# Batch sums of a feature-map attention with values as weights and Gram matrices for its key sums, and a re-searched hand order of the jobs

## The chip, the cores and the metric

The program runs on one core of a Trainium2 chip: TensorE (PE; its weight loads are listed apart, as PEld), VectorE (DVE), ScalarE (ACT), GpSimd (POOL) and SyncE (SP, which issues DMAs). The metric is the device time of one execution in microseconds. Each kernel is executed several times and the median counts; on one core the slowest core is the only one.

## The reference

Two blocks run one behind the other, for 4 batches of 1088 rows. The first is an attention without softmax over features phi, the outer product of two 8-wide sketches of a row; the second is a causal attention with 4 experts, of which each row uses two.

```python
def phi(x):
    a = np.einsum('rd,bhsd->bhsr', S1, x)
    b = np.einsum('rd,bhsd->bhsr', S2, x)
    return np.einsum('bhsi,bhsj->bhsij', a, b).reshape(*x.shape[:-1], r * r)
q_p, k_p = (phi(q), phi(k))
kv = np.einsum('bhsf,bhsd->bhfd', k_p, v)          # 64 x 32 per head
z = np.sum(k_p, axis=2)                            # 64 per head
num = np.einsum('bhsf,bhfd->bhsd', q_p, kv)
den = np.einsum('bhsf,bhf->bhs', q_p, z)[..., None] + 1e-06
x = num / den                                      # heads side by side: 1088 x 128
...
for e in range(E):                                 # 4 experts
    scores = scale * (x @ wq[e]) @ (x @ wk[e]).T   # causal
    a = softmax(scores)
    ye = a @ (x @ wv[e]) @ wo[e]
    out += (weight of e for the row, top 2 of x @ w_gate) * ye
```

All of it is float32. The sum z of a head's features is the 8x8 matrix of the sums over rows of a_i * b_j, and b is the row times S2, so z needs only sums over rows of products of two sketches.

## The kernel before

The kernel is a list of 1284 jobs (a `job(...)` call gives a name, the engines that may do it, what it reads, makes and holds). The order of the jobs is not worked out in the program: a table `ORDER` names them one after the other, with a letter for the engine where there is a choice, and `Plan.run` emits the instructions in that order. Each engine runs its own instructions in that order, so the table is the program's schedule; buffers go round in it too (`pools`: 4 pairs of PSUM banks called `pair`, 6 working tiles `w`, 3 feature tiles `fp`, 2 turned score tiles `AT` and so on).

The jobs of one batch, with the lines that the prediction speaks of:

- Loads of k, q and v, turned by DVE (`turn k`, `turn q`).
- `sketch k` (L523): 32x32 weights from the tables SK, 288 columns moving, 16 tiles of PE's array at a time. Where the weights hold both sketches of the split tables side by side, one pass over the data is enough and a job `join` adds the parts (batches 2 and 3); for batch 1 the tables are used one after the other and nothing is joined. `back` turns the sketches (DVE), `features` (L537, POOL or DVE) multiplies them out to 64 features per head.
- `sums` (L627): for each of 9 blocks of 128 rows and each of 4 heads one matmul with the 128x64 features as weights and 33 columns of v (the 33rd is 1.0 and gives z). `keep sums` copies kv and z to SBUF. `expand` (POOL) spreads z, `fifth` (L768) turns z into an 8-column table that makes the denominator a part of `sketch q`, and `repeat sums` (L762) puts kv into all four row groups of `kvr`. So `sketch q` of a batch stands behind the batch's whole sum. Constants for this (`pick8`, `rep4`, `rep16`, `repeat S2` on L362) are made at the start.
- `sketch q`, weights by the denominator on POOL and DVE, features, `turn f` (L805, DVE), then `numer` (L827), which gives x turned; `keep x`, `turn rows`, store and fetch of x through HBM.
- `logits` (L878, batch 0 L884) and the choice of experts on DVE; masks go through HBM (`store masks`, `fetch masks`) and land in `mb`.
- `query` (L1066), `base` and `pick` (L1079, DVE) give the chosen queries `qs` for three groups of tiles (6, 6 and 5 tiles of 64 rows); `score` (L1104) and `take` (L1116), `exp` (ACT), `guard`, `invert`, `weigh` (L1147, POOL), `turn A` (L1152, DVE) give a tile's weights; `sum V` (L1180) adds them up for a whole group with 32x128 weights, four row tiles of the array at a time; `keep V`, `patch V`, `spread V` choose the experts' parts and `out` (L1301, L1251, L1277) projects.

Batch 0 differs: its attention is done by rows (`project`, `sums 0`, L619, `turn qf`, L666, `numer 0`, L692), and it is the only work there is at the start. `spread v` copies its values into the layout of the sums (L193, ACT and POOL).

PE's matmuls use its array in different shapes: whole (128x128: queries, scores, outputs, transposes), 32x128 (sum V, repeat sums), 128x64 (sums, fifth), 128x32 (logits), 32x32 (sketches, numer). A float32 matmul of the program is two passes in the trace, so the counts of the trace are twice those of the code.

## Time and profile before

| what | value |
|---|---|
| median of 3 runs | 262.74 us (262.19 to 263.94) |
| the profiled execution's span | 261.8 us, 9228 instructions |
| PE busy | 254.9 us (97%), 3811 matmul passes |
| DVE busy | 208.4 us (80%), 529 instructions |
| POOL busy | 157.5 us (60%) |
| ACT busy | 105.6 us (40%) |
| granted clock of PE | 0.9 or more in all 40 slices of the span |

The profiled execution is one of its own; its span runs from the first to the last instruction, and the runs' times hold a little more around it (the median is 0.94 us above the span). A stretch of PE that is counted as busy may still hold short waits, since matmuls are pipelined.

### The profile page before, as it was taken

The page shows a single profiled execution, that of the slowest core. Times are in us where ns is not written, and L with a number is a line of the kernel's source. Part 1 is how long each engine was busy: PE and PEld are TensorE (multiplying, and loading weights), DVE is VectorE, ACT ScalarE, POOL GpSimd, SP SyncE. Part 2 cuts the span into 40 slices and gives each one's busy share as a digit, 9 for nine tenths or more (in the row PEclk, how much of TensorE's full clock was granted, in tenths as well). Part 3 has the DMA queues.
Part 4 walks back from the last instruction along what each step waited for, and adds up shares of the span by engine and source line. Part 5 has one row for each costly group of instructions (what it writes and reads, how often), then busy time and mean ns, then how long its engine had stood idle before and what let it go on. Part 6 is the DMA issues. An engine that isn't in the chain of part 4 may idle for free.

```text
span 261.8 us, 9228 instructions
## 1 busy us (share of the span) xinstructions
PE 254.9 (97%) x3811; PEld 192.2 (73%) x3811; DVE 208.4 (80%) x529; ACT 105.6 (40%) x279; POOL 157.5 (60%) x266
## 2 busy tenths in 40 slices
PE   7899999999999999999999999999999999999995
PEld 2787666646958887665897986666689875589994
DVE  5778999999998996998887497998994388893442
ACT  3453354757242225532814044635514215723120
POOL 5546776899578716597467682366273842542642
PEclk9999999999999999999999999999999999999999
DMA  7978689891467275906044685003370379240012
GB/s 149 212 122 186 112 207 168 158 146 20 73 135 166 67 184 114 148 4 183 3 84 83 143 167 120 4 3 90 93 120 4 96 141 238 47 96 3 5 30 59
DMA packets 87739, 27.35 MB, mean 104 GB/s; under 512 B 58576, under 2 KB 87056, under 8 KB 87696
## 3 DMA queue, kind: packets, MB, share of 16 engines
q1 hardware_dynamic: 85184, 26.15, 50.7%
q10 hardware_dynamic: 2512, 0.61, 1.0%
q8 instruction: 30, 0.49, 0.8%
q14 instruction: 13, 0.11, 0.2%
HBM read 22.22 MB, written 4.52 MB: 102 GB/s over the span
## 4 chain that ended last, share of the span: by engine, by line
PE 84%; DMA 8%; DVE 5%; POOL 1%; issue 1%; SPq 0%; ACT 0%; DVEq 0%; POOLq 0%; ACTq 0%
PE pair L1180 28%; PE pair L1104 24%; PE pair L1066 9%; PE pair L1301 7%; DMA mb<-md 4%; PE pair L1251 3%; PE pair L523 2%; PE pair L827 2%; DMA in<-in_q_dram 2%; DMA w<-in_v_dram 2%; PE pair L627 2%; DVE w L1116 1%; PE pair L1277 1%; DVE fp L805 1%; PE pair L619 1%; PE pair L692 1%
## 5 line engine op out<-in xcount | busy, mean ns | idle before, releaser
L1147 POOL TENSOR_SCALAR w<-w,rs,sh 128x256 f32<-128x256 f32 (+14 forms) x68 | 56.8, 840 | 34.4 <-DVE rs L1143 32.8
L1104 PE MATMUL pair<-xT,qs 128*128 128x320 f32 (+9 forms) x216 | 74.0, 478 | 0.4 <-DVE qs L1079 0.4
L1132 ACT ACTIVATE w<-w,mx 128x64 f32<-128x64 f32 (+15 forms) x68 | 52.4, 772 | 45.8 <-DVE mx L1116 40.6
L1116 DVE CUSTOM_DVE_ANT_0 w<-pair,mask 128x64 f32<-128x64 f32 (+14 forms) x68 | 48.3, 723 | 15.4 <-PE pair L1104 13.0
L1104 PEld LDWEIGHTS pair<-xT,qs 128*128 128x128 f32 x216 | 38.8, 190 | 25.9 <-issue 11.1
L1152 DVE STREAM_TRANSPOSE AT<-w 128x320 f32<-128x320 f32 (+15 forms) x68 | 51.2, 762 | 3.4 <-POOL w L1147 3.0
L1180 PEld LDWEIGHTS pair<-AT,xra 32*128 32x128 f32 x1136 | 41.6, 185 | 4.6 <-issue 2.0
L1180 PE MATMUL pair<-AT,xra 32*128 32x160 f32 (+5 forms) x1136 | 44.9, 303 | 0.0
L1207 POOL TENSOR_TENSOR agg<-agg,mb 128x768 f32<-128x768 f32 (+1 forms) x22 | 34.0, 1559 | 3.4 <-DVE agg L1203 2.0
L1066 PE MATMUL pair<-xT,Mq 128*128 128x384 f32 (+1 forms) x96 | 34.0, 475 | 0.0
L193 ACT COPY agg<-pair 128x384 f32<-128x384 f32 (+1 forms) x31 | 13.2, 463 | 45.5 <-PE pair L1180 44.0
L1180 PEld LDWEIGHTS pair<-AT,xrb 32*128 32x128 f32 x752 | 26.4, 185 | 2.4 <-issue 2.2
L1180 PE MATMUL pair<-AT,xrb 32*128 32x160 f32 (+5 forms) x752 | 28.0, 289 | 0.0
L1140 POOL TENSOR_SCALAR rs<-zs 128x1 f32<-128x1 f32 x32 | 6.8, 214 | 34.0 <-ACT w L1132 23.5
L1066 PEld LDWEIGHTS pair<-xT,Mq 128*128 128x128 f32 x96 | 17.3, 190 | 10.3 <-issue 3.2
L1079 DVE COPY_PREDICATED qs<-mb,pair 128x768 f32<-128x768 uint16 (+1 forms) x24 | 23.1, 962 | 1.5 <-ACT qs L193 0.3
L537 POOL TENSOR_TENSOR fp<-w 128x576 f32<-128x576 f32 x19 | 22.6, 1209 | 1.6 <-DVE w L527 1.1
L1301 PEld LDWEIGHTS pair<-Mo,agg 128*128 128x128 f32 x168 | 20.6, 192 | 2.4 <-issue 0.5
L1301 PE MATMUL pair<-Mo,agg 128*128 128x128 f32 x168 | 21.4, 277 | 0.0
L193 ACT COPY qs<-pair 128x384 f32<-128x384 f32 (+1 forms) x21 | 9.2, 463 | 19.5 <-PE pair L1066 14.2
L1203 DVE COPY_PREDICATED agg<-mb,pair 128x384 f32<-128x384 uint16 (+1 forms) x24 | 12.7, 557 | 4.8 <-ACT agg L193 4.4
L1132 ACT ACTIVATION_READ_ACCUMULATOR w<-w,mx 128x1 f32 x68 | 12.8, 189 | 0.0
(179 smaller groups left out, 297.2 us busy)
## 6 DMA issues: line engine op xcount, KB each, us to landing
xra<-xd SPq DMA_DIRECT2D x16, 192.0 KB, 5.2
xrb<-xd SPq DMA_DIRECT2D x16, 192.0 KB, 5.4
xrc<-xd SPq DMA_DIRECT2D x16, 160.0 KB, 5.0
mb<-md SPq DMA_DIRECT2D x4, 576.0 KB, 7.4
mb<-md SPq DMA_DIRECT2D x4, 480.0 KB, 4.4
mb<-md SPq DMA_DIRECT2D x6, 288.0 KB, 4.3
in<-in_k_dram SPq DMA_DIRECT2D x12, 136.0 KB, 3.4
in<-in_q_dram SPq DMA_DIRECT2D x3, 544.0 KB, 5.6
```

The source lines that it names most:

```text
L193: (nc.scalar.copy if eng == "ACT" else VEC[eng].tensor_copy)(o, i)
L537: VEC[e].tensor_tensor(out=f, in0=a[:, :, None, R : 2 * R].to_broadcast([128, j1 - j0, R, R]), in1=a[:, :, 0:R, None].to_broadcast([128, j ...
L1066: nc.tensor.matmul(plan[ps[x]][:, y, 0:w], Mq[:, ((1, 2), (0, 3))[x][y]], plan[xT][:, 64 * t0 : 64 * t1], start=True, stop=True)
L1079: nc.vector.copy_predicated(chosen(), rows(c), rows(plan[ps[x]]))
L1104: nc.tensor.matmul(plan[p][:, y, 0 : c1 - c0], plan[qs][:, 128 * t : 128 * t + 128], plan[xT][:, c0:c1], start=True, stop=True)
L1116: nc.vector.tensor_tensor_reduce(out=o, in0=src, in1=msk, scale=-1.0, scalar=mx[:, b, i, x - 1 : x] if x else 3e38, op0=ALU.add, op1=ALU.m ...
L1132: nc.scalar.activation(out=a, in_=a, func=ACTF.Exp, bias=mx[:, b, i, last : last + 1], scale=-1.0, accum_out=zs[:, b, i : i + 1])
L1147: nc.gpsimd.tensor_scalar(out=a, in0=a, scalar1=rs[:, b, i : i + 1], scalar2=plan[("sh", b)][:, i : i + 1], op0=ALU.mult, op1=ALU.mult)
L1152: nc.vector.transpose(dst[:, 0 : keys // 32, t], plan[A][:, 0:keys].rearrange("p (j s) -> p j s", s=32))
L1180: nc.tensor.matmul(plan[Vk[g // 2]][:, g % 2, lo : 32 * nt], plan[(f"xr{j // 12}", b)][rows, j % 12], a[rows, j, lo:], start=(j == 0), sto ...
L1207: nc.gpsimd.tensor_tensor(out=a, in0=a, in1=plan[mb][:, 2 * x : 2 * x + 2, 0:w], op=ALU.mult)
L1301: nc.tensor.matmul(plan[p][0:m, 0, 128 * x : 128 * x + 128], plan[agg][:, e, 128 * x : 128 * x + m], Mo[:, e], start=(e == 0), stop=(e == ...
```

## The change

The sums of batches 1 to 3 are done the other way round. `kv` takes 32 columns of v as weights and 64 features as moving columns, four heads at a time in the four column groups of the array. z no longer comes from it: `gram` multiplies the sketches of k with themselves (weights 32 columns, 8 moving columns per head and row block), `tables` turns the result into the denominator's table with a constant SB, and `sketch q` waits for these two only, not for the sum. `repeat kv` takes kv in two halves per head. Batch 1's `sketch k` becomes the one-pass form with a `join`. The constants for the old way go; SB is made from SD on POOL and DVE.

```diff
-        def sums(m):
-            t = plan[kvb][:, :, 0 : D + 1]
+        def sums():
             kp = plan[fps["k"]].rearrange("p (j h f) -> p j h f", h=H, f=R * R)
             for j in range(NJ):
-                for x in range(2):
-                    h = 2 * m + x
-                    nc.tensor.matmul(t[64 * x : 64 * x + 64, m], kp[:, j, h], plan[vp][:, j, h, :],
+                for h in range(H):
+                    nc.tensor.matmul(plan[kvb][32 * h : 32 * h + 32, 0, 0 : R * R], plan[vp][:, j, h, 0:D], kp[:, j, h],
                                      start=(j == 0), stop=(j == NJ - 1))
+        def gram():
+            a = parts_ab("k")
+            for j in range(NJ):
+                for h in range(H):
+                    nc.tensor.matmul(plan[zb][32 * h : 32 * h + 32, 0, 0:R], a[:, h, j], a[:, h, j, 0:R], start=(j == 0), stop=(j == NJ - 1))
...
+            job(f"gram {b}", "PE", 0.58, lambda e: gram(), [("ab", "k", b, 0), ("ab", "k", b, 1)], ("gram", b), [ab["k"], zb], mode="L", rank=at - 0.1)
...
         def repeat_sums():
-            for r in range(4):
-                rows = slice(32 * r, 32 * r + 32)
-                nc.tensor.matmul(plan[rep[r // 2]][:, r % 2, 0 : 2 * D], rep4[rows].rearrange("p g f -> p (g f)"),
-                                 plan[kvs][rows, :, 0:D], start=True, stop=True)
+            for h in range(H):
+                rows = slice(32 * h, 32 * h + 32)
+                for i in range(2):
+                    nc.tensor.matmul(plan[rep[h // 2]][:, h % 2, 32 * i : 32 * i + 32],
+                                     plan[kvs][rows, i].rearrange("p g f -> p (g f)"), ident[rows, rows], start=True, stop=True)
         def fifth():
-            for m in range(2):
-                for s in range(2):
-                    nc.tensor.matmul(plan[rep[0]][64 * m : 64 * m + 64, 0, 128 : 128 + R], S2r[:, s].rearrange("p x d -> p (x d)"),
-                                     zx[:, m], start=(s == 0), stop=(s == 1))
+            for s in range(2):
+                for h in range(H):
+                    nc.tensor.matmul(plan[zb][32 * h : 32 * h + 32, 1, 0:R], SB[:, s, 32 * h : 32 * h + 32], plan[zt],
+                                     start=(s == 0), stop=(s == 1))
...
-        job(f"expand {b}", "POOL", 0.35, lambda e: expand(), [("kvs", b), "pick8"], ("zx", b), [kvs], rank=at)
...
-            sketches("k", at, lambda: SK[:, 0:32] if b == 1 else None, (), lead_fp)
+            sketches("k", at, lambda: None, (), lead_fp)
```

The table `ORDER` is new from the first line on; its first words before and after:

```diff
-0 1 2 3 4 78 79 83 15a 80 45 21a 48 46 10a 81 90 53b 52b 91 54b 50 25b 18a 49 55b 5b 12a 14a 51 82 84 87 85 86 94 64
+0 1 2 3 4 76 77 81 15a 78 45 21a 48 46 10a 79 88 53b 52b 89 54b 50 25b 18a 49 55b 5b 12a 14a 51 13b 9a 11b 65 80 27b
```

What the table does to PE's and ACT's order is shown at three places.

The first is PE's order at the sums of batch 2. Before, the logits of batch 1 (L878), the sums of batch 2 (L627) and the sum V of batch 0's middle group (L1180):

```order
L1104 MATMUL pair_63<-xT_84,qs_97 128x448 x2
L878 MATMUL pair_64<-xT_85,wg 32x288 x4
L627 MATMUL pair_65<-vp_70,fp_77 64x33 x36
L1180 MATMUL pair_66<-AT_98,xra_86 128x192 x2
L1180 MATMUL pair_63<-AT_98,xra_86 128x192 x2
```

After, gram (L610), two scores (L1088), tables (L753), logits (L862), kv (L601) and sketch q (L499):

```order
L610 MATMUL pair_64<-w_73 32x8 x36
L1088 MATMUL pair_63<-xT_85,qs_98 128x480 x2
L753 MATMUL pair_64<-zt_82,SB 32x8 x8
L862 MATMUL pair_65<-xT_86,wg 32x288 x4
L601 MATMUL pair_66<-fp_79,vp_70 32x64 x36
L499 MATMUL pair_64<-in_68,skx_84 32x288 x8
L499 MATMUL pair_63<-in_68,skx_84 32x288 x8
```

The sums' 36 matmuls of 64 weight columns have become 36 of gram and 36 of kv, both in 128x32 form, beside the logits that have this form too; the sketch of q follows at once, where before that whole sum V, L762 and L768 lay between.

The second is PE's order in the sum V of batch 0's last group. Before, a score of batch 1 (L1104) stands inside it:

```order
L1180 MATMUL pair_65<-AT_99,xrb_87 128x160 x2
L1180 MATMUL pair_64<-AT_99,xrb_87 128x160 x2
L1104 MATMUL pair_63<-xT_85,qs_95 128x384
L1180 MATMUL pair_65<-AT_99,xrb_87 128x160 x2
L1180 MATMUL pair_64<-AT_99,xrb_87 128x160 x2
```

After, the same score (128x384) and two queries (L1050) stand ahead of it and the sum (L1164) is in one piece:

```order
L1088 MATMUL pair_64<-xT_86,qs_96 128x64
L1088 MATMUL pair_63<-xT_86,qs_96 128x192
L1088 MATMUL pair_66<-xT_86,qs_96 128x384
L1050 MATMUL pair_65<-xT_86,Mq 128x384 x2
L1164 MATMUL pair_64<-AT_100,xra_87 128x160 x2
L1164 MATMUL pair_63<-AT_100,xra_87 128x160 x2
```

The two changes of the array's shape around the single score are gone. Along the whole of PE's order, neighbours of different shape are 80 before and 62 after; from `numer 1` (the first rows of L827, now L811) to the end they are 50 and 38.

The third is the start. PE before, from the first numerators (L692) to the last logits of batch 0 (L884), with sketch k of batch 1 (L523), the weight products (L401), transposes (L707) and a query (L1066):

```order
L692 MATMUL pair_65<-kvz_80,fp_79 64x66 x12
L523 MATMUL pair_64<-in_68,SK 32x288 x8
L523 MATMUL pair_66<-in_68,SK 32x288 x8
L523 MATMUL pair_64<-in_68,SK 32x288 x8
L523 MATMUL pair_66<-in_68,SK 32x288 x8
L707 MATMUL pair_65<-ident,w_75 128x128 x3
L692 MATMUL pair_63<-kvz_80,fp_79 64x66 x12
L692 MATMUL pair_64<-kvz_80,fp_79 64x66 x12
L884 MATMUL pair_66<-xT_84,wg 32x192 x4
L401 MATMUL pair_65<-AT_98 128x128 x4
L401 MATMUL pair_63<-AT_98 128x128 x4
L707 MATMUL pair_64<-ident,w_75 128x128 x3
```

After, from the middle of that place (sketch k is now two rows) to the last logits (L868), with gram of batch 1 (L610):

```order
L693 MATMUL pair_63<-ident,w_76 128x128 x3
L678 MATMUL pair_65<-kvz_80,fp_78 64x66 x12
L678 MATMUL pair_64<-kvz_80,fp_78 64x66 x12
L868 MATMUL pair_66<-xT_85,wg 32x192 x4
L377 MATMUL pair_63<-AT_99 128x128 x4
L693 MATMUL pair_65<-ident,w_76 128x128 x3
L693 MATMUL pair_64<-ident,w_76 128x128 x3
L610 MATMUL pair_66<-w_71 32x8 x36
L377 MATMUL pair_63<-AT_99 128x128 x4
L868 MATMUL pair_65<-xT_85,wg 32x192 x4
L868 MATMUL pair_64<-xT_85,wg 32x160 x4
```

Sketch k has lost its second half, while gram of batch 1 and one of the two products have moved in ahead of the last logits. ACT's order at the copies of batch 0's values (`vp`, which L619 waits for), before:

```order
L193 COPY w_73<-pair_63 128x320
L193 COPY S2r<-pair_64 64x2x32 x2
L193 COPY vp_70<-w_72 64x4x9x32
L193 COPY w_74<-pair_65 128x192
L193 COPY w_74<-pair_66 128x384
```

and after:

```order
L194 COPY w_73<-pair_63 128x320
L194 COPY w_74<-pair_64 128x192
L194 COPY vp_70<-w_72 64x4x8x32
L194 COPY vp_70<-w_72 64x4x9x32
L194 COPY w_74<-pair_65 128x384
```

The copy of rows 64 to 127 (8x32 per head), which POOL did, now stands on ACT ahead of the other.

Two more moves of the table matter. Between `numer 1` and `numer 2` PE no longer has the output projections of batch 0's middle group (3 jobs, L1301), two queries of batch 1 and the scores of its tiles 7 and 11; they stand behind `numer 2` now. And all eight `features` jobs of q in batches 2 and 3 are POOL's now; DVE did five of them. On SP, `fetch masks` of batch 0 stands behind one `fetch x` and one `store x` that it was ahead of or beside.

## Rows read from the trace of the kernel before

**Rows 1.** The page, busy time, share of the span and instructions of each engine.
```profile
PE 254.9 (97%) x3811; PEld 192.2 (73%) x3811; DVE 208.4 (80%) x529; ACT 105.6 (40%) x279; POOL 157.5 (60%) x266
```

**Rows 2.** Windows: busy time of each engine in four stretches, us from the span's start.
```profile
core 0: us, PE busy (x) PEld busy (x) DVE busy (x) ACT busy (x) POOL busy (x), PEclk, DMA share, GB/s
29.90:52.40 22.50, 21.79 (x324) 14.91 (x321) 21.46 (x61) 11.22 (x37) 16.82 (x43) 1.00 0.87 159
52.40:101.00 48.60, 48.60 (x803) 36.80 (x814) 44.90 (x109) 19.21 (x51) 35.29 (x53) 1.00 0.60 116
101.00:157.90 56.90, 56.90 (x948) 43.78 (x960) 46.01 (x112) 22.79 (x62) 39.42 (x57) 1.00 0.48 98
157.90:258.60 100.70, 100.66 (x1416) 77.62 (x1415) 72.41 (x176) 38.77 (x100) 48.75 (x71) 1.00 0.34 72
```

**Rows 3.** Waits of PE's matmuls behind the first 10 us: us in total, times, longest.
```profile
PE pair L619 <- POOL vp L193: 0.9, 1, 0.9
...
PE pair L1104 <- DVE qs L1079: 0.4, 1, 0.4
PE pair L827 <- DVE w L527: 0.3, 1, 0.3
```

**Rows 4.** Chain that ended last, batches 1 and 2: start us, us, what.
```profile
52.37 2.16 PE pair L827 x42
...
63.21 2.22 PE pair L627 x72
...
70.67 0.22 PE pair L762 x4
...
72.67 0.34 PE pair L768 x8
...
97.44 1.78 PE pair L1301 x16
...
100.08 0.89 PE pair L1301 x8
100.97 1.48 PE pair L827 x38
```

**Rows 5.** The same chain: sketches with two tables and one, numerators of batch 0.
```profile
19.16 1.53 PE pair L523 x63
...
21.16 1.56 PE pair L692 x48
...
105.47 0.70 PE pair L523 x32
```

**Rows 6.** The same chain: 384 columns in whole-array form, inside such work, and between sums.
```profile
84.40 0.65 PE pair L1066 x2
...
91.56 0.84 PE pair L1104 x2
```

**Rows 7.** First passes of sum V (L1180) behind a query, 85.8 to 86.1 us: ns min/median/max.
```profile
L1180 PE MATMUL pair<-AT,xra x7: 294/398/398, 85.8 to 86.1; 32*128 32x160 f32 x7
```

**Rows 8.** ACT's timeline at the copies of batch 0's values.
```profile
10.44 1.17 ACT L193 COPY vp<-w 64x1152 f32<-64x1152 f32 x1
```

**Rows 9.** POOL's timeline at the same place.
```profile
11.09 1.83 POOL L193 COPY vp<-w 64x1024 f32<-64x1024 f32 x1 [1.22 <-DMA w<-in_v_dram]
```

**Rows 10.** DVE's timeline from 32 to 53 us, four of its pieces.
```profile
32.12 0.69 DVE L494 STREAM_TRANSPOSE in<-in 128x512 f32<-128x512 f32 x1
...
42.67 0.88 DVE L1079 COPY_PREDICATED qs<-mb,pair 128x640 f32<-128x640 uint16 x1 [0.24 <-DMA mb<-md]
...
49.31 0.92 DVE L1116 CUSTOM_DVE_ANT_0 w<-pair,mask 128x768 f32<-128x768 f32 x1
...
51.58 1.41 DVE L527 STREAM_TRANSPOSE w<-pair 128x576 f32<-128x576 f32 x2
```

**Rows 11.** Lines: the features on POOL and on DVE, busy us, mean ns of one.
```profile
L537 POOL TENSOR_TENSOR fp<-w 128x576 f32<-128x576 f32 x19 | 22.6, 1209 | 1.6 <-DVE w L527 1.1
...
L537 DVE TENSOR_TENSOR fp<-w 128x576 f32<-128x576 f32 x5 | 3.9, 802 | 0.8 <-POOL w L801 0.8
```

More of the change, by code (lines that the diff above doesn't have):

```diff
@@ L70 @@
+1281 1127b 1128 1123a 1129 1280 1130 1131 1132a 1136b 1137a 1134b 1133b 1135b
 """.split()
@@ L374, with keep_tables, widen_tables @@
-    job("keep S2", ("ACT", "DVE"), (2 * a_us(64), 2 * d_us(64)), lambda e, t=("ps", "S2"): keep_s2(e, t), ["S2p", "pick8"], "S2r",
-        [("ps", "S2")], rank=-29)
+    def keep_tables():
+        nc.gpsimd.tensor_copy(plan[("skx", 1)], SK[:, 0:32])
+    wide = ("w", "tables")
+    def widen_tables():
+        a = plan[wide][:, 0:256].rearrange("p (x h y) -> p x h y", x=2, h=H)
+        nc.gpsimd.memset(a, 0.0)
+        nc.gpsimd.tensor_copy(a[:, :, :, R : 2 * R], SD[:, :, :, R : 2 * R])
+    job("skx", "POOL", 0.25, lambda e: keep_tables(), ["SKW"], "skx", [("skx", 1)], rank=-31)
@@ L377, in one_hot @@
+    job("widen S2", "POOL", 0.6, lambda e: widen_tables(), ["SD"], "S2w", [wide], rank=-30)
+    job("turn S2", "DVE", 0.18 + 0.265, lambda e: nc.vector.transpose(SB.rearrange("p x y -> p (x y)"), plan[wide][:, 0:256]), ["S2w"], "SB",
+        [wide], rank=-29)
     def one_hot():
@@ L640, in prepare @@
                 [("fp", "k" + "+" * y, b, 0), ("vp", b), "const"] + [("kv0", b)] * y, ("kv", b) if y else ("kv0", b), [fps["k"], vp, kvb], mode="M", rank=at + 0.01 * y)
-        for m in range(0 if early else 2):
-            job(f"sums {b}.{m}", "PE", 1.3, lambda e, m=m: sums(m), [("fp", "k", b, m), ("vp", b), "const"],
-                ("kv", b), [fps["k"], vp, kvb], mode="M", rank=at)
-        kvs = ("kvs", b)
+        kvs, zt = ("kvs", b), ("zt", b)
+        if not early:
+            job(f"gram {b}", "PE", 0.58, lambda e: gram(), [("ab", "k", b, 0), ("ab", "k", b, 1)], ("gram", b), [ab["k"], zb], mode="L", rank=at - 0.1)
+            job(f"keep gram {b}", ("ACT", "DVE"), (a_us(8), d_us(8)), lambda e: copy(e, plan[zt], plan[zb][:, 0, 0:R]), [("gram", b)],
+                ("zt", b), [zb, zt], rank=at - 0.1)
+            job(f"kv {b}", "PE", 1.06, lambda e: sums(), [("fp", "k", b, 0), ("fp", "k", b, 1), ("vp", b), "const"],
+                ("kv", b), [fps["k"], vp, kvb], mode="L", rank=at)
         if early:
@@ L779, in attend_turned @@
-        job(f"repeat sums {b}", "PE", 0.25, lambda e: repeat_sums(), [("kvs", b), "rep4"], ("rep", b), [kvs, *rep], mode="V", rank=at)
-        job(f"fifth {b}", "PE", 0.3, lambda e: fifth(), [("zx", b), "S2r", ("rep", b)], ("fif", b), [rep[0]], mode="M", rank=at)
-        job(f"keep fifth {b}", ("ACT", "DVE"), (a_us(8), d_us(8)), lambda e: keep_fifth(e), [("fif", b), "rep16"], ("skx", b), [rep[0], skx], rank=at)
+        job(f"tables {b}", "PE", 0.2, lambda e: fifth(), [("zt", b), "SB"], ("fif", b), [zt, zb], mode="L", rank=at)
@@ L782, in attend_turned @@
+        job(f"keep fifth {b}", ("ACT", "DVE"), (a_us(8), d_us(8)), lambda e: keep_fifth(e), [("fif", b), "skx"], ("skx", b), [zb, skx], rank=at)
+        job(f"repeat kv {b}", "PE", 0.3, lambda e: repeat_sums(), [("kvs", b), "ident"], ("rep", b), [kvs, *rep], mode="V", rank=at)
         for x in range(2):
```

147 lines of the change are left out of this document (59 added, 88 removed).

## The prediction

> **What bounds the kernel now.** I read the busy times first. PE is busy for 254.9 of 261.8 us, DVE for 208.4 [rows 1], and a share alone doesn't say where the one or the other decides, so the windows come next [rows 2]: from 52.4 us to 258.6 us PE is busy in every window but for 0.04 us, while DVE stands at 44.9 of 48.6 us, then 46.0 of 56.9, then 72.4 of 100.7. From 29.9 to 52.4 us it is DVE that is full (21.46 of 22.50) and PE that has gaps. Third, PE's waits [rows 3]: behind the first 10 us its matmuls waited 0.9 us for the copy of batch 0's values, 0.4 us for chosen queries and 0.3 us for the transposes ahead of `numer 1`, and for nothing after that. So there are two parts. Up to about 54 us the end is set by DVE, DMAs and copies, with PE filling; from then on one microsecond of PE work is one microsecond of time, as long as DVE and POOL keep ahead. The clock is 1.00 throughout [rows 2], so no cost changes with it.
>
> **The sums of batches 2 and 3 (PE).** Before, one batch pays 2.22 us for `sums`, 0.22 us for `repeat sums` and 0.34 us for `fifth` [rows 4]: 2.78 us for 88 passes. After, it has 72 passes of kv, 72 of gram, 16 of tables and 16 of repeat.
> - kv: 64 columns move. The nearest row is the numerators of batch 0, 66 columns, two tiles at a time: 48 passes in 1.56 us [rows 5], 65 ns for two. If four tiles run beside one another as two do, 18 rounds of 65 ns are 1.17 us.
> - gram: 8 columns move, which no row shows at this width. `sums` moves 33 and takes 62 ns for two passes (2.22 / 36), hardly less than the 65 ns of twice the columns; so it is the loading of 64 weight columns that counts there, and 32 should take half: 18 x 31 ns = 0.56 us, say 0.6. From above, 72 passes at the pace of the sketches (32 in 0.70 us, 22 ns each [rows 5]) would be 1.58 us.
> - tables: twice the passes of `fifth`, half the weight columns: 0.3 us (0.25 to 0.5). repeat: twice the passes of `repeat sums` with the same 128 weight columns, 0.44 us.
> Sum 2.51 us, a gain of 0.27 per batch; I take 0.3, for two batches 0.6. Ends: all four groups by weight loads alone, 0.56 + 0.56 + 0.25 + 0.44 = 1.8 us (a gain of 1.0 each); or both large ones at 22 ns a pass, 1.58 + 1.58 + 0.5 + 0.44 = 4.1 us (a loss of 1.3 each).
>
> **Fewer changes of PE's shape.** Two passes of 384 columns cost 0.65 us among whole-array work and 0.84 us where they stand between two pieces of sum V [rows 6]: leaving the row-tiled shape costs 0.19 us. Entering it, the first passes last 398 ns instead of 294 [rows 7], at least 0.10 us. I take 0.2 us for either way; other pairs of shapes have no row of their own, between 0 and 0.2. Of the 18 changes that go, 12 lie behind `numer 1`, where PE decides: 12 x 0.2 = 2.4 us (1.2 to 2.4). The 6 in the first part are not counted.
>
> **The start.** Sketch k of batch 1 falls from 1.53 us with two tables to the 0.70 us of batch 3's [rows 5]. Against it, gram of batch 1 (0.6 us and a change of shape) now stands ahead of batch 0's last logits, and the sums of batch 0 start later: POOL copied half of the values in 1.83 us from 11.09 us [rows 9] beside ACT's 1.17 us [rows 8]; now ACT does both behind the same DMA, 11.0 + 1.05 (1024 of 1152 columns) + 1.17 = 13.2 us instead of 12.9. -0.83 + 0.8 + 0.3 is no gain at the logits, so masks and picks come as before. `repeat S2` and the constants lie ahead of that DMA and cost nothing either way.
> From there DVE is the bound, and it has less to do before `numer 1`: one turn of q (0.69 us, done earlier) and tile 11's take (0.92) go [rows 10], with two small copies, and tile 10's take, slightly shorter, comes in. The numerator of batch 1 took 2.16 us where batch 2's took 1.48 [rows 4], because its second PSUM pair came free only with the last turned sketch, at 52.99 us [rows 10]; in the new order that sketch is turned long before. This 0.7 us is what I count at the end of `numer 1`. Ends: -0.7 (a loss, if the later copies and gram do delay the logits) and +1.9 (if DVE's 1.2 us come through as well). The masks of the third group no longer decide anything: DVE waited for them at 42.67 us [rows 10], and its pick now stands behind the takes of group two; so the `fetch masks` behind another fetch and store on SP cost nothing unless they slip by more than 5 us.
>
> **What keeps pace.** Between `numer 1` and `numer 2` PE loses work to the stretch behind: three projections 2.67 us [rows 4], two queries 1.3 us and the scores of tiles 7 and 11, 512 and 768 columns, 2.2 us at the pace of [rows 6]; in all 6.1 us. With the 0.7 us of the numerator, 0.3 of the sums and two changes of shape fewer, PE has 48.6 - 7.5 = 41.1 us there. DVE has 44.9 us, less three `features` at 0.80 [rows 11] and some 0.7 of other pieces: 41.8. POOL has 35.3, plus the three at 1.21 [rows 11]: 38.9. Three engines at 95% and more of one stretch don't run without waits; also gram holds one of the four PSUM pairs until the table is copied. I put down 0.8 us of new waits on PE, with 0 and 6 as ends. The other edits lie under slack: the wider `keep sums` and the copy of gram on ACT (19.2 of 48.6 us busy), the join of batch 1 on POOL before it has scores to weigh. Without that slack they'd cost under 1 us together.
>
> **The sum** is -0.6 - 2.4 - 0.7 + 0.8 = -2.9 us: the profiled execution's span of 261.8 would become 258.9. The median of the runs is 0.94 us above that span, so the forecast is 262.74 - 2.9 = 259.8 us.
>
> **Rivals.** *Passes have a price of their own.* If each of the new short passes costs the 22 ns of the sketches [rows 5], a batch's 176 passes take 3.87 us, 1.1 more than before. Against it: the sketches move 288 columns on sixteen tiles, gram 8 columns on four. Then +2.2 instead of -0.6: 262.6 us.
> The Trainium skill's page "TensorE: Matmul & The Clock Gate" ("Wait — 56ns, not 53.3ns?") speaks for this rival: start-to-start of matmuls never falls below about 25 ns, however few columns move. By it 176 passes would be 4.4 us (an estimate from the page) and the time 263.6 us. The trace's 22 ns per pass [rows 5] already lies below it, so the floor seems to hold for one tile and not across tiles that run side by side.
> *The order gives back what it saves.* The changes of shape saved turn into waits, because longer pieces of one kind leave DVE without scores and then flood it: 2.4 us come back, 262.2 us. For it: [rows 2], the three loads above. Against it: with 80 changes PE waited 0.7 us in all for DVE [rows 3], and behind `numer 2` DVE has 15 to 25% of slack.
> *Slower: the stretch before `numer 2` doesn't shrink.* `spread V` of batch 0's second group stands on POOL behind a `keep V` that is late in DVE's row; the weigh of tile 13 stands behind it on POOL, its turn on DVE behind that, and the last group's sum V and `numer 2` behind the turn. If this keeps the stretch at its 48.6 us while 6.1 us of PE work still come after, the time is 262.74 + 6.1 - 0.7 - 0.3 (batch 3's sums) - 2.0 (the 10 changes of shape saved behind `numer 2`) = 265.8 us. Each microsecond of this chain beyond 42 us adds one; from 45 us on the change is a loss.
>
> **Chances.** Forecast 0.60, passes 0.08, give-back 0.16, stretch 0.16. No change can be told within 1% (2.6 us: 260.1 to 265.4). The forecast's own range, 257.5 to 261.5, lies mostly below 260.1: 0.47 faster, 0.13 the same. The passes give 0.07 the same and 0.01 slower, the give-back 0.14 the same and 0.02 slower, the stretch 0.16 slower. Together 0.47, 0.34, 0.19. The range goes from 256.8 (the start's and the sums' good ends) to 265.0, short of most of the last rival.
>
> **What would show it.** kv's 72 passes in about 1.2 us and gram's in 0.6; `numer 1` ended near 53.8 us and `numer 2` begun near 95; no PE wait of more than 0.5 us behind 54 us, and 12 fewer first passes of the longer kind. Wrong would be: gram or kv above 1.5 us; a wait of PE for tile 13's turned weights or for PSUM pairs behind takes; `numer 1` later than 53.8 us; or a last projection that starts no earlier although PE never waited, which would mean the changes of shape cost less than rows 6 and 7 say.

## The result, and the profile after

The changed kernel is slower: 265.89 us median of 8 executions (265.16 to 268.75), the kernel before 263.50 us beside it (262.19 to 264.65); the ratio is 1.0114 with a 95% interval of 1.008 to 1.0148, some 3 us. Forecast were 259.8 us, with a range up to 265.0. (Ratios leave disturbed executions out, so they can differ from the quotient of two medians.) The profiled execution has a span of 264.5 us against 261.8, and that is 2.7 us of the difference; a further half microsecond lies outside the spans: in the executions beside these runs time and span differ by 1.7 us for the kernel before and by 2.27 for the changed one (medians).

The page of the changed kernel, busy times; they answer to [rows 1].

```profile
PE 253.8 (96%) x4039; PEld 190.7 (72%) x4039; DVE 208.4 (79%) x526; ACT 107.1 (40%) x282; POOL 161.6 (61%) x259
```

PE has 1.1 us less to do and the span is 2.7 us longer: PE stands idle more. Between its first and its last matmul its gaps sum to 6.1 us, before to 2.3; 6.1 - 2.3 - 1.1 = 2.7.

Windows from numerator to numerator (`numer 1` starts at 54.2, `numer 2` at 98.2, `numer 3` at 157.1 us), and last a piece of the front at half clock:

```profile
core 0: us, PE busy (x) PEld busy (x) DVE busy (x) ACT busy (x) POOL busy (x), PEclk, DMA share, GB/s
0.00:54.20 54.20, 49.03 (x727) 33.38 (x727) 45.55 (x131) 25.78 (x69) 38.58 (x82) 0.97 0.89 171
54.20:98.20 44.00, 42.17 (x854) 31.97 (x859) 38.82 (x98) 17.95 (x50) 32.64 (x51) 1.00 0.52 105
98.20:157.10 58.90, 58.90 (x1036) 44.35 (x1040) 48.30 (x116) 22.75 (x62) 40.12 (x59) 1.00 0.35 85
157.10:261.20 104.10, 103.73 (x1445) 81.03 (x1444) 75.24 (x180) 40.50 (x103) 50.26 (x68) 1.00 0.35 79
...
30.30:33.60 3.30, 3.30 (x35) 1.51 (x5) 2.68 (x6) 0.69 (x1) 2.72 (x11) 0.50 0.29 77
```

Beside [rows 2], where `numer 1` starts at 52.37, `numer 2` at 100.97 and `numer 3` near 157.9 us: the front is 1.85 us longer, the stretch up to `numer 2` 4.6 us shorter, the next 2.0 longer, the last 3.4 longer. Behind `numer 1`, DVE and POOL have room everywhere (38.8 and 32.6 of 44 us). For 3.3 us from 30.3 us on PE runs at half clock, 1.2 GHz; that stretch follows a wait of 1.75 us.

PE's waits; they answer to [rows 3].

```profile
PE pair L996 <- DVE cTa L960: 1.7, 1, 1.7
PE pair L610 <- issue: 1.6, 1, 1.6
PE pair L652 <- DVE fp L556: 1.6, 1, 1.6
PE pair L247 <- DVE idle L240: 1.2, 1, 1.2
PE pair L1088 <- DVE rs L1127: 0.4, 1, 0.4
```

The last but one is the warm-up, as before. Ahead of it, from the bottom up: the first features of q at 11.7 us (the kernel before waits 0.9 us there, on the values), gram of batch 2 for something that no semaphore shows ("issue"), and the widening of the masks for the turned choices. The last line is the picks of batch 3, at 190.8 us (the line that it names is DVE's next instruction behind the second pick).

**The first wait: DVE beside POOL.** DVE's and POOL's timelines at 24 us:

```profile
24.11 0.18 DVE L895 TENSOR_TENSOR ch<-ch 128x12 f32<-128x12 f32 x1
24.21 1.19 DVE L896 TENSOR_TENSOR ch<-ch 128x12 f32<-128x12 f32 x1
25.32 1.20 DVE L897 TENSOR_TENSOR ch<-ch 128x6 f32<-128x6 f32 x1
26.45 0.16 DVE L898 TENSOR_TENSOR ch<-ch 128x6 f32<-128x6 f32 x1
```

```profile
21.92 4.58 POOL L513 TENSOR_TENSOR fp<-w 128x576 f32<-128x576 f32 x4
```

Two comparisons of 6 and 12 elements last 1.2 us, where their neighbours last 0.17. POOL makes the four features of k1 in one go, 1.145 us each, so the third ends at 25.36 and the fourth at 26.50 us: each long comparison ends with one of them. In the kernel before POOL had made three and paused. The turned choices come 2.1 us later by it, and PE, whose query projections now stand behind them, has nothing else. The first pick of batch 0 needs these projections; it starts at 34.84 us, and in the kernel before it started at 30.06:

```profile
30.06 2.17 DVE L1079 COPY_PREDICATED qs<-mb,pair 128x768 f32<-128x768 uint16 x2
```

```profile
34.84 2.17 DVE L1063 COPY_PREDICATED qs<-mb,pair 128x768 f32<-128x768 uint16 x2 [0.80 <-ACT qs L194]
```

The kernel before has one such operation too, a product of the choices that lasts 1.14 us and ends, at 29.7 us, with POOL's fourth feature; but these are the choices of the later tiles:

```profile
28.57 1.14 DVE L927 TENSOR_TENSOR c<-c 128x22 bf16<-128x22 bf16 x1
```

**The second wait: PE's own instructions.** PE's timeline at gram of batch 2:

```profile
54.22 1.57 PE L811 MATMUL pair<-fp,kvr 32*32 32x288 f32 x64
55.94 0.70 PE L610 MATMUL pair<-w 128*32 128x8 f32 x63 [0.15 <-DVE agg L1187]
58.28 0.26 PE L610 MATMUL pair<-w 128*32 128x8 f32 x9 [1.65 <-issue]
```

PE stops after 63 of 72 passes for 1.65 us. The DMA queues of 55.4 to 58.2 us have one line that is not data (packets, MB, share of 16 engines), and the page has the whole of it, below:

```profile
q8 instruction: 1, 0.02, 2.9%
```

```profile
q8 instruction: 31, 0.51, 0.9%
```

31 transfers of 16 KB for 4039 passes and as many weight loads are one for every 260 instructions, and they go with PE's instructions: three begin between 55.4 and 63.2 us, among rows of short passes, and two between 174 and 194 us, where passes are long. So this queue is taken to bring PE's own program. One transfer began at 55.45 us and took 1.3 us; PE went on 1.5 us behind its end. The 64 passes of the numerator and 63 of gram are 254 instructions in 2.4 us.

The traces of all the runs below bear this out. They have 17 stops of 0.3 us or more that are put down to "issue", and in each PE goes on 2.4 to 3.0 us after such a transfer began (1.2 to 1.8 us after its end). The kernel before has 30 transfers and no such stop.

**What the new sums cost.** From the chain that ended last, batches 2 and 3:

```profile
55.94 0.70 PE pair L610 x53
...
58.28 0.26 PE pair L610 x9
...
60.35 0.24 PE pair L753 x16
...
61.10 1.00 PE pair L601 x72
...
65.77 0.60 PE pair L747 x16
...
109.71 0.69 PE pair L610 x58
...
110.94 0.13 PE pair L753 x16
...
118.29 1.14 PE pair L601 x72
```

Gram is 0.7 us (forecast 0.6), kv 1.0 to 1.14 (1.17), tables 0.13 to 0.24 (0.3), but repeat 0.5 to 0.60 (0.44; in batch 3 it stands in pieces between passes of a sum of V). Batch 2 takes 2.8 us with gram's tail, as much as the 2.78 us of [rows 4], and batch 3 takes 2.45 us where the same chain of the kernel before has 2.73. So the sums save PE 0.3 us in one of the two batches and nothing in the other, where the stop cuts gram in two.

### The profile page after: what moved, and what is told of

Same layout as the page of the kernel before. It is cut to its first block, busy times and chain, and to the rows that moved or that the text cites. A ratio compares the mean times of both kernels' runs of the same rounds, so it can differ in the third digit from the quotient of the medians.

```text
span 264.5 us, 9662 instructions
## 1 busy us (share of the span) xinstructions
PE 253.8 (96%) x4039; PEld 190.7 (72%) x4039; DVE 208.4 (79%) x526; ACT 107.1 (40%) x282; POOL 161.6 (61%) x259
## 4 chain that ended last, share of the span: by engine, by line
PE 81%; DVE 8%; DMA 5%; issue 2%; ACT 2%; POOL 1%; SPq 1%; DVEq 0%; POOLq 0%; ACTq 0%
PE pair L1164 29%; PE pair L1088 21%; PE pair L1050 8%; PE pair L1285 6%; PE pair L1235 3%; DMA xra<-xd 2%; PE pair L247 2%; DMA mb<-md 2%; PE pair L499 2%; DVE qs L1063 1%; PE pair L811 1%; PE pair L1261 1%; PE pair L652 1%; PE pair L678 1%; DVE w L1100 1%
## 5 line engine op out<-in xcount | busy, mean ns | idle before, releaser
L1131 POOL TENSOR_SCALAR w<-w,rs,sh 128x128 f32<-128x128 f32 (+13 forms) x68 | 55.7, 825 | 36.5 <-DVE rs L1127 32.7
L1116 ACT ACTIVATE w<-w,mx 128x512 f32<-128x512 f32 (+14 forms) x68 | 52.5, 772 | 52.8 <-DVE mx L1100 48.0
L1088 PE MATMUL pair<-xT,qs 128*128 128x384 f32 (+11 forms) x216 | 73.1, 478 | 0.4 <-DVE rs L1127 0.4
L1136 DVE STREAM_TRANSPOSE AT<-w 128x192 f32<-128x192 f32 (+16 forms) x68 | 50.7, 759 | 8.7 <-POOL w L1131 8.7
L1100 DVE CUSTOM_DVE_ANT_0 w<-pair,mask 128x768 f32<-128x768 f32 (+15 forms) x68 | 48.3, 727 | 9.5 <-PE pair L1088 8.8
L1088 PEld LDWEIGHTS pair<-xT,qs 128*128 128x128 f32 x216 | 38.0, 190 | 24.2 <-issue 8.7
L1164 PEld LDWEIGHTS pair<-AT,xra 32*128 32x128 f32 x1136 | 42.0, 185 | 4.9 <-DVE mx L1100 2.0
L1164 PE MATMUL pair<-AT,xra 32*128 32x160 f32 (+5 forms) x1136 | 44.7, 302 | 0.0
L1050 PE MATMUL pair<-xT,Mq 128*128 128x384 f32 (+1 forms) x96 | 35.4, 488 | 0.2 <-DVE rs L1127 0.2
L513 POOL TENSOR_TENSOR fp<-w 128x576 f32<-128x576 f32 x24 | 27.9, 1178 | 0.8
L1164 PE MATMUL pair<-AT,xrb 32*128 32x160 f32 (+5 forms) x752 | 27.6, 287 | 0.0
L1164 PEld LDWEIGHTS pair<-AT,xrb 32*128 32x128 f32 x752 | 26.8, 185 | 0.4 <-issue 0.3
L1050 PEld LDWEIGHTS pair<-xT,Mq 128*128 128x128 f32 x96 | 17.9, 197 | 12.6 <-issue 3.6
L194 DVE COPY agg<-pair 128x384 f32<-128x384 f32 (+1 forms) x15 | 7.9, 526 | 13.1 <-PE pair L1164 12.4
L1124 POOL TENSOR_SCALAR rs<-zs 128x1 f32<-128x1 f32 x28 | 6.0, 214 | 18.5 <-ACT w L1116 13.4
```

The lines of the kernel that those rows point to most:

```text
L194: (nc.scalar.copy if eng == "ACT" else VEC[eng].tensor_copy)(o, i)
L513: VEC[e].tensor_tensor(out=f, in0=a[:, :, None, R : 2 * R].to_broadcast([128, j1 - j0, R, R]), in1=a[:, :, 0:R, None].to_broadcast([128, j ...
L1050: nc.tensor.matmul(plan[ps[x]][:, y, 0:w], Mq[:, ((1, 2), (0, 3))[x][y]], plan[xT][:, 64 * t0 : 64 * t1], start=True, stop=True)
L1088: nc.tensor.matmul(plan[p][:, y, 0 : c1 - c0], plan[qs][:, 128 * t : 128 * t + 128], plan[xT][:, c0:c1], start=True, stop=True)
L1100: nc.vector.tensor_tensor_reduce(out=o, in0=src, in1=msk, scale=-1.0, scalar=mx[:, b, i, x - 1 : x] if x else 3e38, op0=ALU.add, op1=ALU.m ...
L1116: nc.scalar.activation(out=a, in_=a, func=ACTF.Exp, bias=mx[:, b, i, last : last + 1], scale=-1.0, accum_out=zs[:, b, i : i + 1])
```

## The experiments

The mended runs build on queries_warmup_masks and on one another; all others start from the changed kernel or from the order before. "Order" is the order of jobs in the table. Each ratio is against executions of the kernel before beside it.

| kernel | median us | ratio (95%) | span profiled |
|---|---|---|---|
| changed | 265.89 | 1.0114 (1.0080 to 1.0148) | 264.5 |
| features_aside | 266.59 | 1.0134 (1.0100 to 1.0167) | 264.2 |
| queries_ahead | 265.33 | 1.0078 (1.0049 to 1.0106) | 263.0 |
| longer_warmup | 267.34 | 1.0156 (1.0116 to 1.0195) | 264.8 |
| all_three | 266.31 | 1.0118 (1.0086 to 1.0150) | 263.5 |
| sums_alone | 268.24 | 1.0143 (1.0094 to 1.0191) | 264.6 |
| masks_early | 268.65 | 1.0162 (1.0115 to 1.0208) | 266.5 |
| queries_warmup_masks | 265.17 | 1.0062 (1.0032 to 1.0092) | 262.2 |
| sums_spread | 267.61 | 1.0161 (1.0128 to 1.0193) | 265.0 |
| old_front | 268.41 | 1.0182 (1.0134 to 1.0230) | 268.0 |
| old_front_masks | 268.68 | 1.0212 (1.0175 to 1.0249) | 266.1 |
| mended | 264.29 | 1.0066 (1.0037 to 1.0096) | 264.7 |
| mended_feature | 264.35 | 1.0074 (1.0041 to 1.0107) | 262.8 |
| mended_filled | 263.93 | 1.0056 (1.0042 to 1.0071) | 262.4 |
| mended_kv_later | 264.84 | 1.0088 (1.0074 to 1.0102) | 262.6 |

**features_aside.**

```diff
 POOL
-features k1.3, k1.0, k1.1, k1.2, exponents 0.0, shares 0.0, exponents 0.1
+features k1.3, k1.0, exponents 0.0, shares 0.0, features k1.1, k1.2, exponents 0.1
```

> The changed kernel with two of POOL's four features of k1 put behind the shares of the first logits, so that POOL no longer works beside DVE's comparisons at 24.2 us. In the changed kernel's trace two of these comparisons last 1.19 and 1.20 us instead of 0.17, each ending with one of POOL's features, and PE then waits 1.75 us for the turned choices. Theory: the two long comparisons come from POOL's instructions; then they fall below 0.25 us, PE's wait falls from 1.75 below 0.3 us, its clock stays at full speed from 30 to 34 us, and the time falls by 1 to 2 us from 265.9. Rival: the comparisons are long for a reason of their own and stay above 1 us, time 265.9. Second rival: they get short, PE's wait goes, but DVE's own work still sets numer 1 at 54.2 us and the time stays within 0.5 us of 265.9.

DVE's timeline of this run:

```profile
23.83 0.18 DVE L896 TENSOR_TENSOR ch<-ch 128x12 f32<-128x12 f32 x1
23.92 0.17 DVE L897 TENSOR_TENSOR ch<-ch 128x6 f32<-128x6 f32 x1
```

and PE's waits:

```profile
PE pair L1050 <- DVE qs L1063: 1.5, 1, 1.5
...
PE pair L1164 <- issue: 1.1, 1, 1.1
PE pair L610 <- issue: 0.9, 1, 0.9
```

The comparisons are short and PE's wait for the choices is gone, so POOL's features made them long. The Trainium skill's page "SBUF — State Buffer" (section "SBUF: two separate sides") has the rule: GpSimd and an operation of VectorE with two operands in SBUF take a shared pair of ports as an exclusive lock, and the other stands for the whole instruction; these runs agree (1.19 us beside POOL, 0.18 without it). The time didn't fall, though (266.59 us), which is nearest to the second rival, although `numer 1` comes 0.8 us earlier. The two features now run at 30 us, so POOL's pieces for q of batch 1 come later, DVE's picks behind them too, and PE waits 1.5 us for a pick instead; `numer 1` starts at 53.4 us, and 1.15 us are lost at a new stop for instructions in a sum of V.

**queries_ahead.**

```diff
 PE
-tables 1, widen 0, widen 1, sketch q1, query 0.0.00, query 0.0.01, query 0.0.10
+tables 1, query 0.0.00, query 0.0.01, widen 0, widen 1, sketch q1, query 0.0.10
```

> The changed kernel with the first two query projections of batch 0 (four passes, 1.3 us at full clock) put ahead of the widening of the masks on PE, where the kernel before had them. Theory: PE then works through most of the 1.75 us in which it waits for the turned choices (wait below 0.6 us), its clock doesn't fall at 30.2 us, the first queries are copied about 4 us earlier, the first pick of batch 0 starts near 33.9 instead of 34.84 us, and the time falls by 0.5 to 1.5 us from 265.9. Rival: picks and numer 1 hang on DVE alone; the wait of PE is only moved, numer 1 starts at 54.2 us again and the time is 265.9.

PE's wait for the choices fell to 0.54 us, its clock stayed up from 30 to 33.6 us, the first pick starts at 33.55 us, and `numer 1` at 53.0 us:

```profile
30.00:33.60 3.60, 3.21 (x55) 1.62 (x56) 2.88 (x9) 1.65 (x4) 2.94 (x11) 1.00 0.38 101
```

The theory held and the gain is at the low end of it: the ratio went from 1.0114 to 1.0078, though the two intervals overlap. The first pick is still 3.5 us later than in the kernel before.

**longer_warmup.**

```diff
-matmul(pair, idle[:, 0:128], idle) for _ in range(2)
+matmul(pair[0:128], idle[:, 0:128], idle[:, 0:128]) for _ in range(8)
```

> The changed kernel with each idle pass of 512 columns at the start replaced by four of 128: as many columns, 42 passes (84 PE instructions) more, nothing else. In the changed kernel PE stops for 1.65 us in the middle of gram of batch 2, at 56.64 us, on no semaphore; a 16 KB transfer of instructions had begun at 55.45 us. Theory: PE waits there for its own instructions, because numerators and gram use them up faster than the transfer brings them; 84 instructions more ahead of it move the transfer to about 54 us, and the wait falls below 0.3 us; the time falls by about 1.5 us to 264.4, unless another dense stretch is now hit. Rival: the stop belongs to gram or to what it reads; then it stays at 1.65 us and the time at 265.9.

The chain of this run at the same place:

```profile
56.26 0.93 PE pair L610 x66
57.19 1.81 PE pair L1088 x4
59.00 0.24 PE pair L753 x16
59.24 0.51 PE pair L862 x8
59.75 0.67 PE pair L601 x48
60.42 0.53 issue
60.95 0.54 PE pair L601 x24
```

The stop in gram is gone with nothing but 84 instructions more at the start: the transfer that began at 55.45 us now begins at 53.67 and is over before gram starts. The next one begins at 57.94 us, and a shorter stop stands in kv. So the stop belongs to the loading and not to gram. The rest of the chain ate the gain: PE now waits 1.5 us for the picks of batch 3 (0.4 in the changed kernel). The masks of batch 3 come by a DMA that can start only when POOL's spread of V lets go of the buffer. In the changed kernel it starts at 184.2 us and takes 4.6 us; in this run it starts at 183.2 us and takes 5.8.

**all_three.** The three edits together.

> The three edits together. If the three waits are what kept the changed kernel from the forecast, the time is 265.9 less 1.75 (wait for the choices), less some 1 (half clock, late picks), less 1.65 (gram) = 261.5, below the kernel before (263.5). If numer 1 hangs on DVE alone, only gram's wait is saved: 264.3. If none of the theories holds: 265.9.

The profiled execution has no stop for instructions, no wait for the choices, full clock, and `numer 3` 2.4 us earlier than the changed kernel. But 1.8 us go to the picks of batch 3, and POOL is late for q1 as in features_aside. PE's gaps sum to 6.0 us, in the changed kernel to 6.1, and the ratio is as it was: what was taken away came back elsewhere.

**sums_alone.** The change without its new order.

```diff
 PE, batch 2
-logits 1.0, sums 2.0, sums 2.1, sum 0.1.0, ..., repeat sums 2, ..., fifth 2
+logits 1.0, gram 2, kv 2, tables 2, sum 0.1.0, ..., repeat kv 2
 POOL
-expand 1
+join k1.0, join k1.1
```

> The new way of the key sums (gram, tables, values as weights, repeat from kv, k1 sketched in one pass and joined) in the order of the kernel before: kv where the second half of the sums stood, gram just ahead of it, tables just behind it, joins behind the turns of k1; every other job in its old place. Theory A (the new sums are a gain, the re-searched order is the loss): the sums save 0.3 us a batch behind numer 1, 0.6 in all, the front gains up to 0.8 by the shorter sketch; 0.5 to 1.5 us under the kernel before, about 262.2 against 263.1. Theory B (the sums themselves are the loss: stops for instructions and waits for tables in each batch): 264 us or more, with PE standing at gram, kv or tables for over 0.5 us.

The time is that of theory B (268.24 us). PE's waits, and the chain of batch 1:

```profile
PE pair L753 <- issue: 2.6, 2, 1.5
...
PE pair L601 <- issue: 0.6, 1, 0.6
```

```profile
28.70 0.72 PE pair L610 x60
29.42 1.04 PE pair L601 x70
30.46 0.13 PE pair L753 x12
30.59 1.49 issue
```

The dense row of short passes stops for its instructions in every batch: 1.49, 1.15 and 0.56 us, 3.2 us in all. The stop of batch 1 is hidden, since `numer 1` starts at 52.4 us as before. The stretches to `numer 2` and `numer 3` are 1.7 and 0.9 us longer than before; without the stops, and without 0.27 us in which PE waits for ACT's copy of gram, each is still 0.3 to 0.4 us longer. So the sums are no gain with the old order either. Why the rest of these stretches grew is not shown.

**masks_early.**

```diff
 POOL
-weigh 2.10, spread V 2.0.0, guard 2.12, spread V 2.0.1
+spread V 2.0.0, spread V 2.0.1, weigh 2.10, guard 2.12
 DVE
-patch V 2.0.0, invert 2.10, take 2.13, turn A 2.10, take 2.12, patch V 2.0.1
+patch V 2.0.0, patch V 2.0.1, invert 2.10, take 2.13, turn A 2.10, take 2.12
```

> The changed kernel with the two spreads of V of batch 2's first group on POOL, and the patch ahead of the second on DVE, put right behind the first patch, ahead of a weigh and a guard; they hold the mask buffer that batch 3's first masks need. In the changed kernel these masks are fetched at 184.0 us and PE waits 0.37 us for the picks at 190.8, where the kernel before fetched them at 178.2. Theory: the fetch comes 2 us earlier or more and PE's wait goes; alone this is worth 0.4 us at most (265.5), more where the rest is earlier. Rival: POOL or DVE lack the time there, and a new wait behind 191 us costs as much: 265.9 or more.

The rival: the wait for the picks is gone, and PE stands 0.9 us for a PSUM pair at 182.8 us instead, behind DVE's turn of tile 10, which waits for POOL. The mean clock was below 0.995 in 5 of 6 executions (0.97 to 0.994). The edit can't explain that, since it moves nothing before 170 us: in the profiled execution `numer 1` starts at 56.3 us, 2.1 us later than in the changed kernel, and from there to the end it takes 210.2 us, as the changed kernel does (210.3). Behind `numer 1` the edit gained nothing. The one execution at full clock took 267.23 us, and no run shows why.

**queries_warmup_masks.**

> Queries ahead, longer warmup and early masks together. By the spans so far: queries_ahead has 263.0 us, of which PE stands 0.7 + 0.6 us for instructions and 0.6 us for the picks of batch 3. If the instructions no longer stop it and the masks come early, the span is 263.0 - 1.9 = 261.1 us and the time about 263.3, as the kernel before (263.1). If one wait only takes the place of another, 264.5 or more.

Between the two: 1.0062, 1.1 us of the span over the forecast for it. PE's gaps sum to 5.0 us.

**sums_spread.** sums_alone with the row pulled apart.

```diff
 PE
-logits 0.2, ..., gram 1, kv 1, tables 1
+gram 1, products1, turn x 0.1, tables 1, ..., logits 0.1, ..., kv 1
-logits 1.0, gram 2, kv 2, tables 2
+gram 2, score 0.13.00, score 0.13.01, logits 1.0, tables 2, kv 2
-query 2.0.11, query 2.0.10, gram 3, kv 3, tables 3
+gram 3, query 2.0.11, query 2.0.10, tables 3, kv 3
 ACT, batch 2
-guard 0.10, exp 0.13, keep gram 2, keep fifth 2
+keep gram 2, exp 0.10, keep fifth 2, guard 0.10, exp 0.13
```

> As sums_alone (new sums, order of the kernel before), but gram, tables and kv no longer stand in one row on PE: gram of batch 1 goes ahead of the second product of weights with its tables behind a turn of x, gram of batch 2 ahead of the two pieces of a score with its tables behind logits, gram of batch 3 ahead of two query projections with its tables behind them. In sums_alone PE stood in these rows for 1.49, 1.42 and 0.56 us on nothing but the loading of its instructions. Theory: it is the density of short passes that outruns the loading; with long passes between them each stop falls below 0.4 us, and since the sums themselves cost PE as much as before (2.8 us a batch by sums_alone) the time is that of the kernel before, within 1 us (263.4). Rival: the stops come wherever these passes stand; 266 us or more.

```profile
PE pair L1164 <- ACT w L1116: 1.8, 1, 1.8
...
PE pair L1088 <- DVE qs L1063: 1.2, 1, 1.2
PE pair L753 <- ACT zt L194: 0.8, 1, 0.8
```

Not one line with "issue" is left, so the same passes, spread apart, don't stop. That it is their density alone isn't shown: a new order also shifts the moments at which the transfers start, and that by itself moved the stop in longer_warmup. Up to the stops of all runs PE got through 70 to 280 instructions from the transfer's start on, and other transfers saw as many as 228 in 2.5 us without one; four of the 17 stops stand in a sum of V, whose passes are longer. But the time is what it was. PE waits 1.8 us ahead of a sum of V: ACT now stands at the copy of tables (`keep fifth`) ahead of the guard of tile 10, which comes 2.0 us later than in sums_alone, and DVE's turn of that tile, which the sum needs, comes behind it. Tables wait for the copy of gram (0.8 us), and a score for its picks (1.2 us). None of the places tried here takes gram free of charge.

**old_front, old_front_masks.** The old order ahead of `numer 1`, the new one from there on; the second with early masks.

> The changed kernel from numer 1 on, but ahead of numer 1 its jobs stand in the order that the kernel before gives them (gram of batch 1 ahead of the second product of weights, its tables behind a turn of x). Theory: the front's new order is what makes numer 1 late (54.2 instead of 52.4 us) and lets the clock fall (0.98 to 0.994 in most runs); with the old order numer 1 starts by 52.9 us, no wait for the turned choices is above 0.6 us, the clock stays at 1.0, and the time falls by 1 to 1.5 us from 265.9, to about 264.7; gram of batch 2 (0 to 1.8 us, as the loading falls) and the masks of batch 3 (0.4 to 1.8 us) still wait. Rival: numer 1 is late by the joins and gram themselves, not by the order: 53.8 us or later, time 265.9.

> old_front with the early masks of masks_early. If the wait for the picks of batch 3 has grown by what the front gained, this saves 0.5 to 1.5 us against old_front: about 263.7. If POOL's order there only moves the wait (0.92 us at 182 us in masks_early), it is old_front's time within 0.5 us.

Both fell: `numer 1` at 54.7 and 53.4 us, with waits of 0.4 to 1.25 us for sketches and takes ahead of it. The back wants k2's sketch, joins and features done by then, and the old front has no room for them. So the new front isn't simply worse; front and back belong together. That is an argument from the two orders; no run took it apart.

**mended, mended_feature.** queries_warmup_masks, and:

```diff
 DVE (mended)
-take 2.13, turn A 2.10, take 2.12, take 2.11
+take 2.13, take 2.12, take 2.11, turn A 2.10
 POOL (mended_feature, besides)
-features k1.2, exponents 0.0, shares 0.0
+exponents 0.0, shares 0.0, features k1.2
```

> queries_warmup_masks with one more edit: DVE turns the weights of tile 10 of batch 2 behind the takes of tiles 12 and 11 and not ahead of them. In that run DVE stood 1.80 us at this turn for POOL's weigh, and PE behind it 0.92 us for a pair of PSUM. Theory: PE's 0.92 us go and nothing takes their place: span 262.2 - 0.9 = 261.3 us, time about 264.2 (265.2 before the edit). Rival: the wait only moves to the sum of V that reads tile 10, time 265.2.

> As mended, with the last of POOL's four features of k1 behind the shares of the first logits (features_aside moved two and made POOL late for the features of q). DVE's second long comparison (1.2 us) goes, PE's wait for the turned choices (0.55 us) too, numer 1 starts 0.3 to 0.8 us earlier than mended's; time about 263.7, as the kernel before (263.4). Rival: POOL's features of q come 1.2 us later by it and numer 1 stays at 53.0 us; time as mended.

In mended the 0.92 us are gone, but a stop of 0.8 us for instructions stands in kv of batch 2 instead. The 264.29 us are near the expected 264.2 by luck: the kernel before ran at 262.70 beside it, and the ratio, 1.0066, is what it was (1.0062). One feature aside changed nothing that can be measured, the rival again. Mended's profile is one of the executions with a low clock:

```profile
14.60:21.40 6.80, 6.80 (x110) 5.48 (x106) 2.48 (x6) 1.59 (x4) 3.65 (x5) 0.50 0.52 127
```

**mended_filled, mended_kv_later.**

```diff
 PE (both)
-project q0+, turn qf 0.0
+project q0+, 24 idle passes of 128 columns, turn qf 0.0
 PE (mended_kv_later, besides)
-logits 1.0, kv 2, sketch q2, score 0.11.01, score 0.11.00
+logits 1.0, sketch q2, score 0.11.01, score 0.11.00, kv 2
```

> mended with 24 idle passes of 128 columns (some 1.3 us) on PE where it waits 1.5 us for the first features of q at 11.3 us. In mended's profile PE's clock is at half from 14.6 to 21.5 us, and in 4 of the 24 executions of mended and mended_feature the mean clock was 0.985 to 0.987 with spans of 264.7 to 265.0 us against a median of 262.0 at full clock; the kernel before never fell in 40. Theory: it is that wait which lets the clock fall; filled, the clock is at or above 0.997 in every execution, and the slowest span falls to 263.5 us or less; the median changes by less than 0.5 us (264.3). Rival: the clock falls after another wait, and some executions are at 0.985 still.

> mended_filled with kv of batch 2 behind the sketch of q and one score (and the load of the next values behind it), not straight behind tables and logits. In mended and mended_feature PE stood 0.81 and 1.08 us in this kv for its instructions. Theory: with 3.6 us of longer passes between them it doesn't stand there; one change of shape more costs 0.2 us; 0.6 to 0.9 us are gained, 263.6 against 264.3. Rival: the stop moves to another row of short passes, or the repeat behind kv waits for the copied sums: 264.3 or more.

Filled, PE's clock was 1.0 in five of six executions and 0.993 in one, and no execution was slower than 264.63 us, where mended reached 266.96. Without the filling 5 of 24 executions (2 of mended, 3 of mended_feature) had fallen to 0.985 to 0.987; of the eleven with it, here and in mended_kv_later, none did. That points to the wait at 11.3 us, but at a rate of 5 in 24 eleven executions without a fall would come by chance about once in 13 times, so it isn't shown. The median moved by 0.4 us, the ratio is 1.0056. The stop in kv stays:

```profile
58.99 0.33 PE pair L601 x24
59.32 0.82 issue
60.14 0.88 PE pair L601 x48
```

With kv moved away, the next row of short passes takes its place, the sketch, and for longer (1.2 us, ratio 1.0088): the rival.

## Why the prediction was wrong, step by step

- *The sum.* Forecast -2.9 us, measured some +3. Up to the start of `numer 1` the forecast left the time as it was (its 0.7 us lie in the numerator itself); it came 1.85 us late. From there to the end of the span it expected 2.9 us less; it was 0.9 more (210.3 against 209.4). Of these 3.8 us, 1.4 are waits (2.2 in place of 0.8), some 1.0 the changes of shape, 0.3 the sums and 0.1 the numerator; about 1 us stays open.
- *Sums, -0.3 us a batch.* Right in batch 3 (2.45 us for 2.73), nothing in batch 2. Gram came out 0.1 us dearer than put down, repeat up to 0.16. The rival on passes (22 or 25 ns each) fell all the same: kv's 72 passes took 1.14 us, 16 ns each, gram's 72 about 0.7 us, 10 ns each. What the passes do cost is their loading, in stops, for which neither forecast nor rival had a term.
- *Changes of shape, 0.2 us each.* Mis-sized, as far as one stretch can tell. Behind `numer 3` the changed kernel has 8 fewer (counted along PE's matmuls: 21 and 13) and 24 passes of projections and 4 of queries more, 2.67 + 1.3 = 4.0 us by [rows 4, 6]. PE's time there grew from 100.7 to 103.7 us without the wait: 0.9 us saved, some 0.12 each, an estimate that rests on the prices of the moved work. For all 12 that is about 1.4 us in place of 2.4, near the lower end that was given.
- *The numerator of batch 1.* Right: 1.57 us in place of 2.16, a gain of 0.6 where 0.7 was put down.
- *The front, no gain at the logits and then a lead.* The first half was right (the first logits start at 22.16 us, before at 22.65). The step that failed is "masks and picks come as before": the choices came 2.1 us late by POOL's features beside DVE's comparisons, and with the queries moved behind them PE had nothing to fill in with, the clock fell behind that wait, and the first pick came 4.8 us late. "So no cost changes with" the clock, which was put at nothing, failed with it: 0.50 for 3.4 us. Putting two queries back brought `numer 1` 1.2 us earlier, 0.4 of them by an earlier first feature in that execution.
- *New waits, 0.8 us.* The size failed, and the place. They were looked for where three engines seemed full, between `numer 1` and `numer 2`. There DVE had 38.8 us to do, not 41.8, and POOL 32.6, not 38.9, since more had been done ahead (POOL 38.6 us up to `numer 1`, before 34.0), and PE waited for neither longer than 0.2 us. The waits that came are 1.75 us (choices), 1.65 (instructions, for which the prediction had no term), 0.7 more at the start and 0.4 (masks).
- *The rivals.* 265.8 us, the number of the slower one, is nearly the time, but not by its mechanism: the stretch up to `numer 2` shrank by 4.6 us, and no chain over POOL's spread of V held it. Nearest in kind is the give-back: from all_three on, what one edit freed was taken by the next wait in line.
- *Two numbers of the prediction.* The good ends of the start and of the sums give 257.2 us, not 256.8, and DVE's slack behind `numer 2` in [rows 2] is 19 and 28%, not 15 to 25. Neither bears on the outcome.

Settled by the runs: the long comparisons come from POOL; the stops go with the loading of instructions, and the same passes set apart don't stop; the sums alone gain nothing. By five edits, three of the order and two of PE's idle passes, the loss shrank from 1.0114 to 1.0056, whose intervals don't touch; how much each of the five gave is within the noise. Open is the other half of the loss: the rest of the front (`numer 1` at 53.1 to 54.1 us in the mended kernels at full clock, before at 52.4), one stop for instructions, what makes a row of passes stop and another not, and the half microsecond outside the span. This last goes with the order of the front: time and span differ by 1.8 us in old_front and old_front_masks, and by 2.1 to 2.3 us in every run with the new front. No version ran faster than the kernel before, so that stays the best.

## What to carry to other kernels

Where PE is full, count a change's instructions and not its columns alone: a row of passes of some 10 ns can empty what has been loaded, and PE then stands for up to 1.65 us on a wait that shows no releaser. Before trusting an order, look at what small DVE operations on a critical chain run beside on POOL, and at what PE can fill in with while it waits; a hand order that has been measured has answers to both built in. Undo single edits only with an eye on the next wait: here it took five together to get half of the loss back.
